# Attention, routed experts and a gated unit on one core: the gated unit's weight joins moved to steps 1 and 5 of an expert unit, the next inputs turned in step 7

## The chip, the core and the metric

The kernel runs on one core of one Trainium2 chip. A core has a matrix engine (TensorE, PE in the views), a vector engine (VectorE, DVE), a scalar engine (ScalarE, ACT), GpSimd (POOL) and a queue engine that issues most transfers (SyncE, SP). Every engine has its own instruction list and works it off in order; it stops where an instruction needs something that another engine or a transfer has not delivered. The metric is the time of one execution on the device in microseconds (us); smaller is better.

## The reference, cut to what matters

The kernel computes three layers on 4608 tokens of width 512. Only the second, with the beginning of the third, is near the change.

```
# 1: attention in chunks of 64 -> x (4608 x 512)
# 2: routed experts, each token goes to one of eight
do_compute = x @ w_skip > 0
e_idx = argmax(x[do_compute] @ w_gate);  gate_w = softmax at e_idx
for e in range(8):
    h = maximum(xc[mask] @ w1[e], 0)           # 512 -> 1024
    y[mask] = gate_w * (h @ w2[e])             # 1024 -> 512
x[do_compute] += y
# 3: gated unit on all tokens
silu = g * sigmoid(g),  g = x @ w_gate;  out = (silu * (x @ w_val)) @ w_out
```

Experts' and gated unit's matmuls are done in three passes: each operand is split into a high part and a low part (`hi`, `lo`), and hi*hi, lo*hi and hi*lo are added up (`mm3`, lines 250 to 252).

## The kernel before, in words

The experts' work is a list of eleven **units**, run one after the other: eight static units (one expert each, up to 272 tokens in two tiles of 128 rows and one of 16) and three dynamic units (128 tokens of an expert that is known only at run time). In order, with the number u: 0, 1, 2 static, 3 dynamic, 4 to 8 static, 9 and 10 dynamic. Unit 0 stands ahead of the loop that the change touches.

A static unit has eight **steps** (`f` = 0 to 7 in the code; the text says step 1 to 8). A step is: twelve matmuls of the first layer for 128 hidden columns into the PSUM tile `hp`; ScalarE takes the positive part as `hh`, VectorE makes the low part `hl` (line 394); then twelve matmuls of the second layer, of the step before, into the four tiles `yt`; then `tick(f)`, which appends side work. The second layer of step 8 is done in step 1 of the following unit. `back()` (in step 3) turns a finished unit's result `yts` on TensorE, and VectorE adds it to the tokens' rows (line 334).

The side work of `tick`, in the order in which it is written:

- `put` (step 4): three scatters of the unit before, issued by GpSimd (line 342).
- `gather(u + 1)` (step 2): the next unit's rows, up to three, issued by GpSimd (line 291).
- `xpose(u + 1)`: those rows are turned on TensorE into `tp` and one `hp` tile (line 322), ScalarE makes `xh`, VectorE `xl` (line 325).
- `pump`: slices of the coming experts' weights are split: ScalarE `whi` (line 148), then VectorE `wlo`, or GpSimd for every fourth slice (line 150). A static unit splits 16 slices, two or three in a step and one in steps 4 and 8. Its loads `st` go through SyncE's queue, in turn, each waiting for one of four buffers.
- `gpump`: one slice of the gated unit's weights, which lie in memory as 64-bit numbers, is **joined**: three VectorE instructions (lines 228, 231, 234) make `cv` from `gst`. `gsplit` then splits `cv`: ScalarE `ghi` (line 202), GpSimd `glo` (line 203). `gfetch` issues the load of the next `gst`, for which there is one buffer. Twelve slices are joined in the static units 1, 2 and 4 to 7, two in each.

`gpump` itself begins with a `gsplit` of whatever was joined before and is not yet split. No planner decides the order: each engine's list is in the order of the calls. Each of the PSUM tiles `hp` has two buffers, used in turn by the steps' first layer, by `back` and by `xpose`, so that a user waits until the one two places earlier has been read.

Of the kernel before, what the change touches and what calls it, by code (L numbers as in the profile page):

```python
# [54 lines left out]
def attention_moe_glu_kernel(  # L55
# [33 lines left out]
    gst = {"slice": 0, "dma": 0, "stage": [], "conv": []}  # L89
# [89 lines left out]
    def chunk_done(c):  # L179
        st["done"] = max(st["done"], c + 1)  # L180
# [18 lines left out]
    def gsplit():  # L199
        if gst["conv"]:  # L200
            w, hi, lo = gst["conv"].pop()
            nc.scalar.activation(out=hi, in_=w.bitcast(F32), func=ACTF.Copy)
            nc.gpsimd.tensor_tensor(out=lo, in0=w.bitcast(F32), in1=hi.bitcast(F32), op=ALU.subtract)
# [61 lines left out]
    def load_perm(u, bases):  # L265
        r = []
        for t, b in enumerate(bases):
            pm = al["pm"](u)
            idx = pm
            if t == 2:  # L270
                src = perm[b:b + REST, ROW - 2:]
                idx = al["pm"](u)[0:REST]
                ins = nc.sync.dma_start(out=idx, in_=src)
                after(ins, scattered)
                pm = pm[rest(u)]
            else:
                src = perm[b:b + P, ROW - 2:] if isinstance(b, int) else perm[bass.ds(b, P), ROW - 2:]
            ins = nc.sync.dma_start(out=pm, in_=src)
            after(ins, scattered)
            r.append([pm, idx])  # L280
        rows[u] = r
# [6 lines left out]
    def gather(u, n=NT + 1):  # L288
        for t, r in enumerate(rows[u]):
            x = al["x"](u) if t < 2 else al["xr"][rest(u)]  # L290
            ins = nc.gpsimd.indirect_dma_start(
                out=x, out_offset=None, in_=X[0:n, :],
                in_offset=bass.IndirectOffsetOnAxis(ap=r[1][:, 0:1].bitcast(U32), axis=0),
                bounds_check=n - 1, oob_is_err=False,
            )
            apart(ins, u)
            r.append(x)
# [12 lines left out]
    def xpose(u):  # L310
        xh, xl = xts[u] = al["xt"](u)
        for t, (_, _, x) in enumerate(rows[u]):
            n = P
            one = ident
            if t < 2:
                p = al["t"](t)
            else:
                p = al["h"](KD * P).rearrange("p (k t) -> p k t", k=KD)
                n = REST
                one = ident[rest(u), rest(u)]  # L320
            for k in range(KD):
                nc.tensor.transpose(p[:, k, 0:n], x[:, k * P:(k + 1) * P], one)
            sl = slice(t * P, t * P + n)
            nc.scalar.activation(out=xh[:, :, sl], in_=p[:, :, 0:n], func=ACTF.Copy)
            nc.vector.tensor_tensor(
                out=xl[:, :, sl], in0=p[:, :, 0:n], in1=xh[:, :, sl].bitcast(F32), op=ALU.subtract
            )
# [623 lines left out]
    with mctx:  # L951
        wb = gpool["b"] = ctx.enter_context(tc.tile_pool(name="wb", bufs=GSLOTS))
        gpool["t"] = ctx.enter_context(tc.tile_pool(name="cv", bufs=2))
        gpool["st"] = mctx.enter_context(tc.tile_pool(name="gst", bufs=1))
        hp_.append(mctx.enter_context(tc.tile_pool(name="hd", bufs=4)))
        ps_h = mctx.enter_context(tc.tile_pool(name="ps_h", bufs=2, space=PSUM))
        ps_y = mctx.enter_context(tc.tile_pool(name="ps_y", bufs=1, space=PSUM))
        ps_t = mctx.enter_context(tc.tile_pool(name="ps_t", bufs=2, space=PSUM))
        warm = io.tile([P, 1], F32, tag="warm", name="warm", bufs=1)
        al.update(  # L960
            t=lambda t: ps_t.tile([P, KD, P], F32, tag="t", name="tp"),
            h=lambda n: ps_h.tile([P, n], F32, tag="h", name="hp"),
            yt=lambda d: ps_y.tile([P, UNIT], F32, tag=f"y{d}", name="yt"),
            ts=lambda: hp_[1].tile([P, 2, UNIT], F32, tag="hd", name="yts"),
            y=lambda t: ps_y.tile([P, DM], F32, tag="y3", name="y"),
        )
        usual = dict(al)
        held = outs[:]
        outs.clear()
        al.update(  # L970
            pm=lambda u: io.tile([P, 2], I32, tag="lpm", name="lpm", bufs=1),
            x=lambda u: gpool["st"].tile([P, DM], F32, tag="st", name="lx"),
            xt=lambda u: [gpool["t"].tile([P, KD, P], F32R, tag="cv", name=nm) for nm in ("lxh", "lxl")],
        )

        total = nc.values_load(tab[0:1, 2 * TAB:], min_val=NDYN, max_val=TAB)
        with tc.For_i(NDYN, total, 1) as j:
            er = nc.values_load(tab[0:1, bass.ds(j, 1)], engines=[mybir.EngineType.SP], min_val=0, max_val=NE - 1)
            br = nc.values_load(
                tab[0:1, bass.ds(j + TAB, 1)], engines=[mybir.EngineType.SP], min_val=0, max_val=PERM - P  # L980
            )
            load_perm("loop", [br])
            gather("loop")
            xpose("loop")
            got = {}

            def getl(kind, h):
                i = (kind, h)
                if i not in got:
                    src = moe_src(er, kind, h)  # L990
                    hi = wb.tile([P, 4, 512], F32R, tag="w", name="wl_hi")
                    lo = wb.tile([P, 4, 512], F32R, tag="w", name="wl_lo")
                    t = wb.tile([P, 4, 512], F32, tag="w", name="wl")
                    nc.sync.dma_start(out=t, in_=src)
                    for k in range(KD):
                        nc.scalar.activation(out=hi[:, k, :], in_=t[:, k, :], func=ACTF.Copy)
                        nc.gpsimd.tensor_tensor(
                            out=lo[:, k, :], in0=t[:, k, :], in1=hi[:, k, :].bitcast(F32), op=ALU.subtract
                        )
                    got[i] = (hi, lo)  # L1000
                return got[i]

            unit_dyn("loop", getl, lambda kind, h: None, None, lambda f: None)()
            put()

        al.update(usual)
        outs.extend(held)
        put()
        gfetch()
        tail = None  # L1010
        for u, (kind, n) in enumerate(units):
            if not u:
                continue
            nxt = u + 1 < len(units)

            def tick(f, u=u, kind=kind, nxt=nxt):
                if f == (3 if kind == "s" else 2):
                    put()
                if f == 1 and kind == "s":
                    gather(u + 1)  # L1020
                if f == (5 if kind == "s" else 3) and nxt:
                    xpose(u + 1)
                if kind == "s":
                    pump(2 + f % 2)
                    if f in (2, 6) and gst["stage"]:
                        gpump(1)
                    if f in (0, 4) and gst["slice"] < 12:
                        gfetch()
                    if f == 4:
                        gsplit()  # L1030
                    if f == 6 and units[u + 1][0] == "d" and u + 2 < len(units):
                        gather(u + 2)
                elif nxt or f < 4:
                    pump(2)
                if u == len(units) - 2 and f == 3:
                    first_rows("a")
                if not nxt:
                    if f == 2:
                        gpool["ahead"] = 2
                        gfetch()  # L1040
                    elif f == 5:
                        xpose("a")
                        gpump(1)
                        nc.scalar.activation(out=warm, in_=ident[:, 0:1], func=ACTF.Sigmoid)
                if f == 3:
                    pre_perm(u + 3)

            fn = unit_static if kind == "s" else unit_dyn
            order = ORDER_S if kind == "s" else ORDER_D
            tail = fn(  # L1050
                u,
                lambda a, h, u=u, order=order: chunk(4 * u + order.index((a, h))),
                lambda a, h, u=u, order=order: chunk_done(4 * u + order.index((a, h))),
                tail, tick,
            )
        tail()
        put()
        gpool["ahead"] = 3
        gfetch()
# [151 lines left out]
```

## Time and profile before

| what | value |
|---|---|
| runs | 1342.19, 1343.88 and 1346.43 us; median 1343.88 |
| profiled execution | 1347.4 us, of it 1345.7 us from the first to the last instruction (the span) |
| TensorE | 1290.9 us busy, 96% of the span |
| VectorE | 647.2 us busy, 48% |
| ScalarE | 417.6 us busy, 31% |
| GpSimd | 256.0 us busy, 19% |
| mean granted TensorE clock | 0.988 |

The profiled execution is 3.5 us over the median. The shares of busy time are means over stages with different limits: up to about 190 us attention, routing and unit 0, from there to about 426 us the units 1 to 10, and then the gated unit. What a wait costs has to be read in its stage.

### The profile page before, as it was taken

What the parts mean: (1) busy time and instruction counts of PE and PEld (TensorE: products, weight loads), DVE (VectorE), ACT (ScalarE), POOL (GpSimd) and SP (SyncE); (2) the same over time, 40 slices, a digit from 0 to 9 for tenths busy, and PEclk for the clock granted to TensorE, in tenths of its full rate; (3) what the DMA queues carried; (4) which work ended last, traced back from release to release, by engine and by line L of the source; (5) the groups of instructions that cost most, each with busy time, mean ns of one, the idle gap of its engine ahead of it and who ended that gap; (6) DMA issues with size and microseconds to landing.
All of it is one profiled execution on the core that took longest, in us unless ns stands there. A gap on an engine that the chain in (4) does not pass through costs nothing.

```text
span 1345.7 us, 23671 instructions
## 1 busy us (share of the span) xinstructions
PE 1290.9 (96%) x9772; PEld 1192.8 (89%) x9772; DVE 647.2 (48%) x1159; ACT 417.6 (31%) x862; POOL 256.0 (19%) x226
## 2 busy tenths in 40 slices
PE   7688899999999999999999999999999999999998
PEld 6566699899997889999999999999999999999997
DVE  6688467687758885232333323332333333232332
ACT  4455345655555333121122212121212112111221
POOL 0156454555545563000000000000000000000000
PEclk9899799999999999999999999999999999999999
DMA  9996356786657441102020110202020100201000
GB/s 333 350 404 249 105 161 212 253 266 231 213 186 255 135 151 30 40 0 48 1 47 1 30 19 1 47 1 48 0 48 0 34 14 0 48 0 39 1 24 17
DMA packets 125904, 136.09 MB, mean 101 GB/s; under 512 B 78359, under 2 KB 81670, under 8 KB 125794
## 3 DMA queue, kind: packets, MB, share of 16 engines
q1 hardware_dynamic: 121090, 124.46, 29.0%
q0 software_dynamic: 4704, 10.10, 2.1%
q8 instruction: 77, 1.26, 0.4%
q14 instruction: 33, 0.27, 0.1%
HBM read 108.05 MB, written 27.17 MB: 100 GB/s over the span
## 4 chain that ended last, share of the span: by engine, by line
PE 76%; DVE 3%; issue 2%; ACT 2%; POOL 1%; DMA 1%; SPq 0%; POOLq 0%; ACTq 0%; DVEq 0%
PE o L252 7%; PE o L251 7%; PE o L250 7%; PE pg L252 7%; PE pg L250 7%; PE pg L251 7%; PE pv L252 7%; PE pv L251 7%; PE pv L250 7%; PE hp L250 2%; PE hp L252 2%; PE hp L251 2%; PE yt L251 2%; PE yt L252 2%; PE yt L250 2%
## 5 line engine op out<-in xcount | busy, mean ns | idle before, releaser
L1152 DVE TENSOR_TENSOR sg<-pg,sg 128x384 f32<-128x384 f32 (+1 forms) x132 | 72.1, 546 | 327.0 <-ACT sg L1151 327.0
L252 PE MATMUL pg<-xh,glo 128*128 128x384 f32 (+1 forms) x528 | 175.5, 332 | 0.0
L250 PE MATMUL pg<-xh,ghi 128*128 128x384 f32 (+1 forms) x528 | 175.1, 332 | 0.0
L1156 ACT ACTIVATE uh<-sg 128x384 fp32r<-128x384 f32 (+1 forms) x156 | 78.1, 500 | 311.9 <-DVE sg L1153 311.9
L251 PE MATMUL pg<-xl,ghi 128*128 128x384 f32 (+1 forms) x528 | 174.8, 331 | 0.0
L250 PE MATMUL pv<-xh,ghi 128*128 128x384 f32 (+1 forms) x528 | 173.9, 329 | 0.0
L251 PE MATMUL pv<-xl,ghi 128*128 128x384 f32 (+1 forms) x528 | 173.9, 329 | 0.0
L252 PE MATMUL pv<-xh,glo 128*128 128x384 f32 (+1 forms) x528 | 173.9, 329 | 0.0
L252 PE MATMUL o<-ghi,ul 128*128 128x512 f32 x432 | 171.1, 396 | 2.2 <-POOL ul L1158 2.2
L250 PE MATMUL o<-ghi,uh 128*128 128x512 f32 x432 | 168.8, 391 | 2.6 <-ACT uh L1156 2.6
L251 PE MATMUL o<-glo,uh 128*128 128x512 f32 x432 | 170.6, 395 | 0.0
L1151 ACT ACTIVATE sg<-pg 128x384 f32<-128x384 f32 (+1 forms) x132 | 63.6, 482 | 311.5 <-PE pg L252 311.5
L1153 DVE TENSOR_TENSOR sg<-pv,sg 128x384 f32<-128x384 f32 (+1 forms) x132 | 72.1, 546 | 118.4 <-PE pv L252 118.3
L1158 DVE TENSOR_TENSOR ul<-sg,uh 128x384 fp32r<-128x384 f32 (+1 forms) x132 | 72.2, 547 | 76.8 <-ACT uh L1156 76.8
L150 DVE TENSOR_TENSOR wlo<-st,whi 128x512 fp32r<-128x512 f32 x117 | 95.5, 844 | 27.2 <-ACT whi L148 23.0
L150 POOL TENSOR_TENSOR wlo<-st,whi 128x512 fp32r<-128x512 f32 x59 | 79.1, 1342 | 135.9 <-ACT whi L148 116.7
L250 PEld LDWEIGHTS pg<-xh,ghi 128*128 128x128 f32 x528 | 99.4, 188 | 5.9
L251 PEld LDWEIGHTS pg<-xl,ghi 128*128 128x128 f32 x528 | 99.3, 188 | 5.7
L148 ACT ACTIVATE whi<-st 128x512 fp32r<-128x512 f32 x176 | 101.8, 627 | 6.1 <-DMA st<-in_moe_w_dram 5.8
L252 PEld LDWEIGHTS o<-ghi,ul 128*128 128x128 f32 x432 | 81.0, 188 | 21.6 <-POOL ul L1158 4.4
L250 PEld LDWEIGHTS pv<-xh,ghi 128*128 128x128 f32 x528 | 99.3, 188 | 0.0
L251 PEld LDWEIGHTS pv<-xl,ghi 128*128 128x128 f32 x528 | 99.3, 188 | 0.0
(180 smaller groups left out, 2503.3 us busy)
## 6 DMA issues: line engine op xcount, KB each, us to landing
st<-in_moe_w_dram SPq DMA_DIRECT2D x88, 512.0 KB
q<-in_qkv_dram SPq DMA_DIRECT2D x35, 768.0 KB
X<-x SPq DMA_DIRECT2D x36, 256.0 KB
out_dram<-os SPq DMA_DIRECT2D x36, 256.0 KB
xr<-X SPq DMA_DIRECT2D x128, 64.0 KB
gst<-in_moe_w_gate_dram SPq DMA_DIRECT2D x12, 512.0 KB
gst<-in_moe_w_val_dram SPq DMA_DIRECT2D x12, 512.0 KB
gst<-in_moe_w_out_dram SPq DMA_DIRECT2D x12, 512.0 KB
```

The source lines that it names most:

```text
L148: nc.scalar.activation(out=hi[:, k, :], in_=stage[:, k % 2, :], func=ACTF.Copy)
L150: eng.tensor_tensor(out=lo[:, k, :], in0=stage[:, k % 2, :], in1=hi[:, k, :].bitcast(F32), op=ALU.subtract)
L250: nc.tensor.matmul(ps, ah, bh, start=start, stop=False)
L251: nc.tensor.matmul(ps, ah, bl, start=False, stop=False)
L252: nc.tensor.matmul(ps, al, bh, start=False, stop=stop)
L1151: nc.scalar.activation(out=u, in_=pg, func=ACTF.Sigmoid)
L1152: nc.vector.tensor_tensor(out=u, in0=pg, in1=u, op=ALU.mult)
L1153: nc.vector.tensor_tensor(out=u, in0=pv_, in1=u, op=ALU.mult)
L1156: nc.scalar.activation(out=uh, in_=u, func=ACTF.Copy)
L1158: eng.tensor_tensor(out=ul, in0=u, in1=uh.bitcast(F32), op=ALU.subtract)
```

## The change

Three of `tick`'s conditions change. The next inputs are turned in step 7 in place of step 6. A slice is joined in steps 1 and 5 in place of 3 and 7. The next slice is fetched in steps 3 and 7 in place of 1 and 5, and the separate `gsplit` goes from step 5 to step 3. Nothing is added or taken away.

```
-                if f == (5 if kind == "s" else 3) and nxt:
+                if f == (6 if kind == "s" else 3) and nxt:
                     xpose(u + 1)
                 if kind == "s":
                     pump(2 + f % 2)
-                    if f in (2, 6) and gst["stage"]:
+                    if f in (0, 4) and gst["stage"]:
                         gpump(1)
-                    if f in (0, 4) and gst["slice"] < 12:
+                    if f in (2, 6) and gst["slice"] < 12:
                         gfetch()
-                    if f == 4:
+                    if f == 2:
                         gsplit()
                     if f == 6 and units[u + 1][0] == "d" and u + 2 < len(units):
                         gather(u + 2)
```

VectorE's list from the turned inputs of unit 6 through the first three steps of unit 7; `hl` are the low parts of the steps, the three `cv` rows are one join. Before:

```order
L325 TENSOR_TENSOR xl<-hp,xh 128x4x16
L150 TENSOR_TENSOR wlo<-st,whi 128x512 x2
L394 SCALAR_TENSOR_TENSOR hl<-hp,hh 128x272
L150 TENSOR_TENSOR wlo<-st,whi 128x512 x2
L228 TENSOR_SCALAR cv<-gst 128x512
L231 SCALAR_TENSOR_TENSOR cv<-gst,cv 128x512
L234 SCALAR_TENSOR_TENSOR cv<-gst,cv 128x512
L394 SCALAR_TENSOR_TENSOR hl<-hp,hh 128x272 x2
L150 TENSOR_TENSOR wlo<-st,whi 128x512 x2
L394 SCALAR_TENSOR_TENSOR hl<-hp,hh 128x272
```

The same place of the changed kernel:

```order
L325 TENSOR_TENSOR xl<-hp,xh 128x4x16
L150 TENSOR_TENSOR wlo<-st,whi 128x512 x2
L394 SCALAR_TENSOR_TENSOR hl<-hp,hh 128x272 x2
L150 TENSOR_TENSOR wlo<-st,whi 128x512 x2
L228 TENSOR_SCALAR cv<-gst 128x512
L231 SCALAR_TENSOR_TENSOR cv<-gst,cv 128x512
L234 SCALAR_TENSOR_TENSOR cv<-gst,cv 128x512
L394 SCALAR_TENSOR_TENSOR hl<-hp,hh 128x272
```

The join stood ahead of the `hl` pair of step 8 and the next unit's step 1; now it stands behind this pair and ahead of the `hl` of step 2. The turned inputs are one step nearer to the unit's end.

GpSimd's list in a unit like 7, from the gather of the next unit's rows on; `wlo` are its shares of the experts' weights. Before:

```order
L291 DMA x<-X,pm 128x512 x2
L291 DMA xr<-X,pm 16x512
L150 TENSOR_TENSOR wlo<-st,whi 128x512
L203 TENSOR_TENSOR glo<-cv,ghi 128x512
L342 DMA X<-x,pm 4609x512 x2
L342 DMA X<-xr,pm 4609x512
L150 TENSOR_TENSOR wlo<-st,whi 128x512
L203 TENSOR_TENSOR glo<-cv,ghi 128x512
L150 TENSOR_TENSOR wlo<-st,whi 128x512 x2
```

The same unit of the changed kernel:

```order
L203 TENSOR_TENSOR glo<-cv,ghi 128x512
L291 DMA x<-X,pm 128x512 x2
L291 DMA xr<-X,pm 16x512
L150 TENSOR_TENSOR wlo<-st,whi 128x512
L203 TENSOR_TENSOR glo<-cv,ghi 128x512
L342 DMA X<-x,pm 4609x512 x2
L342 DMA X<-xr,pm 4609x512
L150 TENSOR_TENSOR wlo<-st,whi 128x512 x3
```

One `glo` now stands ahead of the gathers, and both stand ahead of the scatters; behind the scatters the three shares of `wlo` follow one another.

## Rows read from the trace of the kernel before

**Rows 1.** Busy time by engine in stretches, in us; PEclk is the granted clock.

```profile
190.00:430.00 240.00, 231.98 (x1729) 221.03 (x1727) 172.67 (x263) 133.96 (x282) 122.35 (x98) 0.99 0.70 231
430.00:530.00 100.00, 94.59 (x655) 86.47 (x654) 79.01 (x118) 32.20 (x72) 58.16 (x46) 1.00 0.40 123
```

**Rows 2.** Waits of TensorE from 190 to 430 us: total, times, longest.

```profile
PE yt L251 <- DVE hl L394: 2.8, 5, 0.8
```

**Rows 3.** Timeline of TensorE, unit 7's step 1: start, duration, instruction, idle before it.

```profile
342.85 0.28 PE L252 MATMUL hp<-xh,wlo 128*128 128x272 f32 x1
342.97 0.29 PE L250 MATMUL yt<-hh,whi 128*128 128x272 f32 x1
343.74 0.40 PE L251 MATMUL yt<-hl,whi 128*128 128x272 f32 x1 [0.48 <-DVE hl L394]
343.98 0.29 PE L252 MATMUL yt<-hh,wlo 128*128 128x272 f32 x1
```

**Rows 4.** Timeline of TensorE, unit 4's step 5.

```profile
274.14 0.29 PE L250 MATMUL yt<-hh,whi 128*128 128x272 f32 x1
...
275.49 0.29 PE L252 MATMUL yt<-hh,wlo 128*128 128x272 f32 x1
```

**Rows 5.** Timeline of VectorE from unit 6's turned inputs to unit 7's step 1.

```profile
336.51 0.21 DVE L325 TENSOR_TENSOR xl<-hp,xh 128x64 fp32r<-128x64 f32 x1
...
341.67 1.67 DVE L234 SCALAR_TENSOR_TENSOR cv<-gst,cv 128x512 uint32<-128x512 uint32 x1
343.26 0.78 DVE L394 SCALAR_TENSOR_TENSOR hl<-hp,hh 128x272 fp32r<-128x272 f32 x2
```

**Rows 6.** The tile gst, 190 to 430 us: duration ns min/median/max, first and last start.

```profile
L228 DVE TENSOR_SCALAR cv<-gst x14: 411/416/1118, 202.9 to 428.2; 128x512 uint32<-128x512 uint32 x14
...
L234 DVE SCALAR_TENSOR_TENSOR cv<-gst,cv x14: 691/693/2066, 204.1 to 429.3; 128x512 uint32<-128x512 uint32 x14
```

**Rows 7.** Timeline of VectorE, one join in unit 4.

```profile
270.91 1.12 DVE L228 TENSOR_SCALAR cv<-gst 128x512 uint32<-128x512 uint32 x1 [0.32 <-DMA gst<-in_moe_w_val_dram]
...
272.79 2.07 DVE L234 SCALAR_TENSOR_TENSOR cv<-gst,cv 128x512 uint32<-128x512 uint32 x1
```

**Rows 8.** Timeline of GpSimd beside that join.

```profile
270.37 1.37 POOL L203 TENSOR_TENSOR glo<-cv,ghi 128x512 fp32r<-128x512 f32 x1 [2.20 <-ACT ghi L202]
...
272.98 1.31 POOL L150 TENSOR_TENSOR wlo<-st,whi 128x512 fp32r<-128x512 f32 x1
```

**Rows 9.** Timeline of ScalarE in unit 7, steps 1 and 6.

```profile
345.72 1.15 ACT L148 ACTIVATE whi<-st 128x512 fp32r<-128x512 f32 x2
...
360.22 0.40 ACT L393 ACTIVATE hh<-hp 128x272 fp32r<-128x272 f32 x1 [1.04 <-PE hp L252]
```

**Rows 10.** Timeline of VectorE in unit 7, steps 1 and 5.

```profile
346.37 1.29 DVE L150 TENSOR_TENSOR wlo<-st,whi 128x512 fp32r<-128x512 f32 x2 [2.33 <-ACT whi L148]
...
358.17 1.54 DVE L150 TENSOR_TENSOR wlo<-st,whi 128x512 fp32r<-128x512 f32 x2
```

**Rows 11.** Timeline of TensorE in unit 7: `back` in step 3, `xpose` in step 6.

```profile
350.60 0.60 PE L377 MATMUL hp<-ident,yts 128*16 128x128 f32 x4
...
361.53 1.03 PE L322 MATMUL tp<-ident,x 128*128 128x128 f32 x8
```

**Rows 12.** Timeline of GpSimd in unit 7: gathers, scatters, a share of `wlo`.

```profile
342.95 1.34 POOL L291 DMA_INDIRECT x<-X,pm  x1 [0.16 <-issue]
...
345.91 0.90 POOL L291 DMA_INDIRECT xr<-X,pm  x1 [0.30 <-issue]
...
353.41 1.31 POOL L342 DMA_INDIRECT X<-x,pm  x1 [0.15 <-issue]
...
357.23 1.32 POOL L150 TENSOR_TENSOR wlo<-st,whi 128x512 fp32r<-128x512 f32 x1
```

**Rows 13.** Timeline of SyncE's queue in unit 4: issue of a `gst` load.

```profile
262.92 0.46 SPq L193 DMA_DIRECT2D gst<-in_moe_w_val_dram  x1
```

**Rows 14.** Chain that ended last, 405 to 420 us: a load from issue to landing.

```profile
413.08 4.85 DMA st<-in_moe_w_dram
```

## The prediction

> **What bounds the kernel now.** I read first the busy time by stretch, since the change lies between 190 and 430 us alone. There TensorE is busy 232.0 of 240.0 us at a granted clock of 0.99, and VectorE 172.7 [rows 1]. So TensorE's own work sets this stretch, its instructions are the same after the change, and all that can be won are its waits, some 8 us. Then the waits of TensorE: one group belongs to the units and comes back, five waits of the second layer's second matmul (which reads `hl`) for VectorE, 2.8 us by the view [rows 2]. The others are single events at the stretch's ends, which the change does not touch. Behind the stretch the gated unit has TensorE busy for 94.6 of 100 us [rows 1] and takes over a shift of the stretch's end one to one.
>
> Then the timeline at such a wait. In unit 7's step 1 the matmul on `hh` starts at 342.97, the one on `hl` only at 343.74, and the third at 343.98 [rows 3]. At the usual pitch of 0.125 us (342.85 to 342.97 in the same rows) the third would start 0.25 us after the first. It starts 1.01 after it: the wait costs 0.76 us, more than the 0.48 of idle time that the row shows. Four of the five waits are of this kind, at the beginning of units 2, 6, 7 and 8. The fifth is in unit 4: 275.49 - 274.14 - 0.25 = 1.10 us [rows 4]. **All five: 4 x 0.76 + 1.10 = 4.14 us**, 0.31% of the time, and the most that the change can win.
>
> Last, why `hl` is late. VectorE finishes the turned inputs at 336.72, is then in arrears with `wlo`, and the join's last instruction takes 1.67 us instead of 0.69, so that the `hl` pair begins at 343.26 only [rows 5, 6].
>
> **Unknown that decides: two engines that shut each other out.** The join's instructions take 0.41, 0.69 and 0.69 us when nothing disturbs them [rows 6]. Beside a GpSimd split they don't share, they wait. In unit 4 a first join instruction that began at 270.91, inside a GpSimd split that ended at 271.74, ended at 272.03, 0.3 us behind it. A last one begun at 272.79 ended at 274.86, 0.57 us after the split of 272.98 to 274.29 [rows 7, 8]. So each meeting costs VectorE about 1 us, and the order of GpSimd's list matters as much as that of VectorE's.
>
> The Trainium skill, "SBUF — State Buffer", section "Who interferes with whom", says that a VectorE instruction with two inputs in SBUF contends with a GpSimd one that reads SBUF, that whichever issues first keeps the shared ports for its whole length, and that the other fully blocks. The rows agree that one blocks; but the instruction of 272.79 is recorded 0.19 us ahead of GpSimd's and was nevertheless the one that waited. What the page's order of precedence would make of the sum is the rival "half".
>
> **The change part by part,** on unit 7's times of before.
>
> *Turning in step 7.* Moved behind two groups of twelve matmuls, 24 x 0.125 = 3.0 us. Its matmuls are the same ones. VectorE is then done with `xl` at 336.72 + 3.0 = 339.7, two `wlo` (1.29 for two [rows 10]) bring it to 341.0, and `hl` of step 8, 0.4 long [rows 5], is done near 341.4. TensorE wants it at 342.97 + 0.125 = 343.1. No join stands between any more. The wait is covered by 1.7 us, and the next unit's first matmul at 341.47 finds `xl` ready. **Gain: 0.76 us at the start of units 2, 6, 7 and 8.** In unit 4 the join of step 3 goes too: **1.10 us**.
>
> *Joining in step 1.* From here on TensorE stands 0.76 us earlier than in the rows. ScalarE's two `whi` of step 1 end at 345.72 + 1.15 - 0.76 = 346.1 [rows 9], and `ghi`, the same operation on a tile of the same size (half of 1.15, 0.6 us), now follows at once, to 346.7. VectorE's two `wlo` end at 346.37 + 1.29 - 0.76 = 346.9 [rows 10] and the join begins. But at 346.7 GpSimd begins `glo`, some 1.4 us long (1.37 and 1.32 in [rows 8, 12]), to 348.1. The first join instruction therefore ends some 0.3 us behind it, at 348.4; with 2 x 0.69, gaps, and 0.4 for `hl` (half of 0.78 [rows 5]), step 2's `hl` is done near 350.3. Queued behind it on VectorE stand the next `wlo` and `hl`; waiting for it is TensorE, since the last four transposes of `back`, at 350.60 - 0.76 = 349.84 [rows 11], go into the `hp` buffer of step 2, which is free when that `hl` has read it. The wait is 0.45 us, and starting again costs another 0.1 (from 343.74 to 343.98 in [rows 3] it is 0.24 in place of 0.125); without the meeting it is nothing, with one more of 0.2 to 0.3 it is 0.75. I take 0.6. `back` with a pending `glo` and a join exists in units 2, 5, 6 and 7. **Loss: 4 x 0.6 = 2.4 us**, between 0 and 3.0.
>
> *Joining in step 5.* What is late here is GpSimd's list. Before, the gathers start at 342.95 and end at 346.81, 3.86 us; the scatters start at 353.41 and the split behind them at 357.23, 3.82 us [rows 12]. Now, end to end: `glo` to 348.1 and hand-over to 348.2, gathers to 352.1, a split to 353.5, the second `glo` to 354.9, scatters to 358.75, and the split of 357.23 runs from 358.75 to about 360.3, 1.6 us later than before. VectorE's two `wlo` of step 5 (358.17 to 359.71 before [rows 10]) end about 359.4, and the join's first instruction meets this split: done near 360.7, the second near 361.4. ScalarE begins step 6's slices behind `hh`, which ends at 360.62 [rows 9], some 0.15 earlier now; two `whi` later, at 361.55, GpSimd starts its next split, and the last join instruction meets that one: 361.55 + 1.3 + 0.57 = 363.4, and `hl` of step 6 is done at 363.9. TensorE has no turned inputs here any more, so its step 7 begins at 361.53 - 0.15 = 361.4 [rows 11], and after twelve matmuls, 1.5 us, it wants `hl` at 363.0. **Loss: about 0.95 us** in the units where gathers, `back` and scatters are all there in full: 5, 6 and 7, **2.85 us**. Unit 2 gathers one tile and unit 4 scatters one, so that GpSimd is some 2.6 us earlier; unit 1 has no `back`. I take nothing there.
>
> *Fetching in steps 3 and 7.* The load of step 3 now stands in SyncE's list behind a weight load that waits for a buffer until VectorE has split step 3's first slice, near 355.5, and the join of step 5 wants it at 359.4 to 360.7. A load took 4.85 us from issue to landing at 413.08 [rows 14]; the `gst` issued at 262.92 [rows 13] held VectorE's join up until 270.91 [rows 7], 8.0 us. Issued at 355.9 the first lands at 360.75, just in time; the second at 363.9. The rows don't say which is nearer; I take the first, since it asks no queue of transfers ahead beyond one load, at no cost; by the second `hl` would be done at 366.1, and the wait 3.1 us in place of 0.95. The load of step 7 has about 7 us and is covered.
>
> *Sum:* -4.14 + 2.4 + 2.85 = **+1.1 us** on the profiled 1347.4 us, whose span is 1345.7. That execution is 3.5 us over the median 1343.88, on which I put the same sum: **1345.0 us**. Five waits go, seven smaller or equal ones come.
>
> **The rivals.**
> - *Half: the step 5 meetings don't happen.* If the join's last instruction, begun at 361.45, keeps GpSimd out instead of being kept out, `hl` of step 6 is done at 362.6, before 363.0. -4.14 + 2.4 = -1.7, 1342.1 us. For it: a shift of the two lists by 0.2 us is enough. Against it: the instruction of 272.79, which began first and waited [rows 7, 8]. The page's precedence named above leads to this one.
> - *All gain: the step 1 meeting doesn't reach TensorE either*, because `glo` or the join comes half a microsecond later or earlier than I reckon. -4.14, 1339.7 us. Against it: two engines' lists send `glo` and the join off within 0.2 us.
> - *Slower: the `gst` load of step 3 lands late.* Place: step 5 of units 5 to 7, VectorE idle ahead of line 228. It decides from a landing about 361 us on. At 8.0 us the sum is -4.14 + 2.4 + 3 x 3.1 = +7.6, 1351.5 us; at 6 us, +4 or so. For it: the landing of 8.0 us [rows 7, 13], and the scatters that run in the same 4 us. Against it: the 4.85 us [rows 14].
>
> **How the numbers follow.** A difference of 0.3%, 4.0 us, is about what a measurement of this kernel can tell from none: its three runs lie 4.2 us apart. Chances: waits change place (1345.0, between 1343 and 1347) 0.40; half 0.25; all gain 0.12; late load 0.23. Faster by over 0.3% is most of the upper end of "all gain", 0.09; slower by over 0.3% a good half of the late load, 0.14; within it 0.77. The range 1340.0 to 1350.0 leaves out half of "all gain" and the far end of the late load. The likeliest case alone: 1343 to 1347.
>
> **What would show it.** In the profile after: no wait for `hl` of step 8 at the start of units 2, 6, 7 and 8, and none in unit 4's step 5 (if they are there, the first step is wrong). Waits of 0.4 to 0.75 us at the transposes of `back`, line 377, in units 2, 5, 6, 7. Waits of about 1 us at line 251 in step 7 of units 5, 6, 7, with the join's last instruction at 1.5 us or more beside a GpSimd split. Line 228 idle for `gst` at most a few tenths. What would make the prediction wrong: a landing past 361 us, or meetings that fall otherwise by 0.3 us, since in both places the margin is smaller than that.

## The result: 15 us slower, outside the range

| | before | after |
|---|---|---|
| device time, median of 5 runs | 1342.19 us (1339.98 to 1346.43) | 1357.18 us (1354.09 to 1357.29) |
| ratio to before, 95% interval | 1 | 1.0107 (1.0092 to 1.0121) |
| profiled execution: time, span | 1347.4, 1345.7 us | 1354.09, 1352.3 us |
| first matmul of unit 1 to first matmul of the gated unit | 234.05 us | 247.56 us |

The change costs 15.0 us; 1345.0 was forecast, and the range ended at 1350. The two profiled executions lie only 6.7 us apart, because the attention ahead of the experts, which the change leaves alone, took 6.4 us longer in the profile of before (unit 1 begins there at 192.84, after the change at 186.48). So I compare the stretch from unit 1's first matmul to the first of the gated unit, which holds everything that was moved. Two lines on TensorE's timeline of the changed kernel bound it: start, duration, instruction, idle before it.

```profile
186.48 0.39 PE L250 MATMUL hp<-xh,whi 128*128 128x272 f32 x1 [2.04 <-issue]
...
434.04 0.28 PE L250 MATMUL pgv<-xh,ghi 128*128 128x256 f32 x1
```

It is 13.5 us longer than in the profile of before (192.84 to 426.89). Both kernels were profiled once more (below): 234.46 and 251.02 us, 16.6 apart. The two differences average 15.0 us, which happens to be that of the medians too; what sets the two pairs apart is told with the clock further down. The loss lies in this stretch.

Next the waits of TensorE in it, which answer to [rows 2]: total, times, longest, in the changed kernel.

```profile
PE yt L251 <- DVE hl L394: 8.8, 5, 2.5
PE y L250 <- ACT hth L428: 3.0, 1, 3.0
PE hp L377 <- DVE hl L394: 2.1, 4, 1.5
...
PE hp L250 <- DVE hl L394: 0.5, 1, 0.5
```

The first row looks like the one of before with three times the total, 8.8 in place of 2.8, and again five waits. They are five other waits: none stands at the start of a unit or in unit 4's step 5 any more, and all five are in step 7, in units 2, 4, 5, 6 and 7. One of them, on TensorE in unit 7:

```profile
366.12 0.29 PE L250 MATMUL yt<-hh,whi 128*128 128x272 f32 x1
368.69 0.40 PE L251 MATMUL yt<-hl,whi 128*128 128x272 f32 x1 [2.29 <-DVE hl L394]
368.93 0.29 PE L252 MATMUL yt<-hh,wlo 128*128 128x272 f32 x1
```

Read as [rows 3] were, it costs 368.93 - 366.12 - 0.25 = 2.56 us. VectorE's timeline says what made `hl` late:

```profile
361.25 2.72 DVE L150 TENSOR_TENSOR wlo<-st,whi 128x512 fp32r<-128x512 f32 x2
...
366.40 0.43 DVE L228 TENSOR_SCALAR cv<-gst 128x512 uint32<-128x512 uint32 x1 [2.44 <-DMA gst<-in_moe_w_out_dram]
...
367.59 0.69 DVE L234 SCALAR_TENSOR_TENSOR cv<-gst,cv 128x512 uint32<-128x512 uint32 x1
368.20 0.43 DVE L394 SCALAR_TENSOR_TENSOR hl<-hp,hh 128x272 fp32r<-128x272 f32 x1
```

VectorE stands idle for 2.44 us ahead of the join's first instruction, for the transfer of `gst`; behind it the join runs undisturbed (0.43 and 0.69 are its free durations, [rows 6]), and only then comes the `hl` that TensorE waits for. SyncE's list has the issue of this load, behind two weight loads:

```profile
356.92 2.16 SPq L137 DMA_DIRECT2D st<-in_moe_w_dram  x2
359.13 0.46 SPq L193 DMA_DIRECT2D gst<-in_moe_w_out_dram  x1
```

From 359.13 to 366.40 are 7.3 us, not the 4.85 of [rows 14]. VectorE's waits over the whole stretch show that this is no single case; before, there was one such wait, of 0.3 us:

```profile
DVE cv L228 <- DMA gst<-in_moe_w_val_dram: 3.7, 2, 2.6
DVE cv L228 <- DMA gst<-in_moe_w_gate_dram: 2.5, 2, 1.6
DVE cv L228 <- DMA gst<-in_moe_w_out_dram: 2.4, 1, 2.4
```

Five waits, 8.6 us, against five of TensorE with 8.8.

**The sum from these traces.** The five old waits saved 4.14. The new ones cost, from start to start as in the prediction, 1.52 (unit 2), 0.94 (unit 4), 2.73, 2.55 and 2.56 (units 5, 6, 7): 10.3. The matmuls right behind unit 6's wait took another 1.0 us, at a lower granted clock (further down): 11.3. The transposes of `back` cost 0.35 each in units 5, 6 and 7 and 2.45 in unit 2: 3.5. From unit 8's last `back` to the gated unit's first matmul it takes 28.03 us in place of 25.78: 2.25. Together -4.14 + 11.3 + 3.5 + 2.25 = 12.9 of the 13.5; the other 0.6 I did not assign. For one whole unit the same shows as a pitch: from `back` to `back` 27.5 us before, 29.85, 31.0 and 29.7 after (units 5 to 8).

### The profile page after: what moved, and what is told of

It is laid out like the page before. It is cut to its first block, busy times and chain, and to the rows that moved or that the text cites. A ratio compares the mean times of both kernels' runs of the same rounds, so it can differ in the third digit from the quotient of the medians.

```text
span 1352.3 us, 23663 instructions
## 1 busy us (share of the span) xinstructions
PE 1288.8 (95%) x9772; PEld 1192.5 (88%) x9772; DVE 649.9 (48%) x1159; ACT 418.6 (31%) x862; POOL 254.1 (19%) x226
## 4 chain that ended last, share of the span: by engine, by line
PE 73%; DVE 4%; DMA 3%; issue 3%; ACT 1%; POOL 1%; SPq 0%; DVEq 0%; POOLq 0%; ACTq 0%
PE o L252 7%; PE o L251 7%; PE o L250 7%; PE pg L252 7%; PE pg L250 7%; PE pg L251 7%; PE pv L251 7%; PE pv L252 7%; PE pv L250 7%; PE hp L250 2%; PE hp L252 1%; PE hp L251 1%; PE yt L251 1%; PE yt L252 1%; DVE wlo L150 1%
## 5 line engine op out<-in xcount | busy, mean ns | idle before, releaser
L150 DVE TENSOR_TENSOR wlo<-st,whi 128x512 fp32r<-128x512 f32 x117 | 98.5, 877 | 24.4 <-ACT whi L148 23.4
L252 PEld LDWEIGHTS pv<-xh,glo 128*128 128x128 f32 x528 | 99.3, 188 | 0.0
```

Source lines behind the costliest of these rows:

```text
L150: eng.tensor_tensor(out=lo[:, k, :], in0=stage[:, k % 2, :], in1=hi[:, k, :].bitcast(F32), op=ALU.subtract)
L252: nc.tensor.matmul(ps, al, bh, start=False, stop=stop)
```

## The experiments

The change moves four conditions of `tick`: turning, join, fetch and separate split. The theory after this reading: the load of `gst`, fetched in steps 3 and 7, comes too late for the join of step 5. The rivals: (A) the meetings of VectorE's join with GpSimd's splits make `hl` late, and the wait for the load only takes up time that would be lost anyway; (B) the turning in step 7 does it, since it leaves TensorE nothing to do between `hh` and `hl` of step 6.

**e1: the change, with the fetch where it was before.**

```diff
-                    if f in (2, 6) and gst["slice"] < 12:
+                    if f in (0, 4) and gst["slice"] < 12:
                         gfetch()
```

> The changed kernel with the fetch of the next slice back in steps 1 and 5, right behind the join that frees the buffer, so that the load is issued four steps ahead of its join. Theory (late load: the load issued in step 3 lands about 7 us later, VectorE stands at the join of step 5 and TensorE in step 7): the waits of step 7, 11.3 us in units 2 and 4 to 7 of the changed kernel's trace, go; 1342 to 1346 us, near the kernel before. Rival A (VectorE and GpSimd shutting each other out, as the prediction had it): the step 5 meetings stay, 1345 to 1349 us. Rival B (turning in step 7 is what delays): still 1353 to 1358 us.

Measured: 1346.66 us, 1.0033 (1.0020 to 1.0046) against before. That is outside the theory's range and in A's. One pair of numbers that says in which steps a load is sent off gives back 10.5 of the 15 us (9.9 by the two ratios). The timelines of SyncE, VectorE and GpSimd in unit 7:

```profile
344.70 0.34 SPq L193 DMA_DIRECT2D gst<-in_moe_w_out_dram  x1
```

```profile
352.70 2.69 DVE L150 TENSOR_TENSOR wlo<-st,whi 128x512 fp32r<-128x512 f32 x2
...
356.49 1.67 DVE L234 SCALAR_TENSOR_TENSOR cv<-gst,cv 128x512 uint32<-128x512 uint32 x1
```

```profile
356.33 1.29 POOL L150 TENSOR_TENSOR wlo<-st,whi 128x512 fp32r<-128x512 f32 x1 [1.49 <-issue]
```

The load now leaves 10.6 us ahead of its join (line 228 starts at 355.31), and no wait for it is left on VectorE. What is left is what the prediction described in step 5: the join's last instruction, 1.67 us in place of 0.69, beside a GpSimd split that began at 356.33. It makes TensorE wait in step 7, by 1.02, 1.00 and 1.00 us in units 5, 6 and 7; 0.95 was forecast. So the theory holds for 10.5 us, and A is right too, for some 3 us that appear when the load is on time; after the change the late load hides these meetings, since the join then runs behind the splits. With the 3.5 us at `back` the sum is -4.14 + 3.0 + 3.5 = +2.4; measured +3.9 (2.7 to 6.2 by the interval).

**e2: the change, with eleven of the twelve `gst` loads left out.**

```diff
         while gst["dma"] <= min(gst["slice"] + gpool["ahead"], 35):
             c, k = divmod(gst["dma"], 4)
+            if 0 < gst["dma"] < 12:
+                gst["stage"].append(gst["one"])
+                gst["dma"] += 1
+                continue
...
+            gst["one"] = t
             gst["stage"].append(t)
```

> The changed kernel, in which eleven of the twelve loads of gated slices in the units are left out: all twelve joins read the slice that was loaded first (so part of the gated unit's first weights is left out). Late load: VectorE can't wait for the landing, 1341 to 1345 us, and at most 2 us better than with the early fetch, by what the loads cost on the shared transfers. Rival A: 1345 to 1349 us. Rival B: 1353 to 1358 us.

Measured: 1345.21 us, 1.0019 (1.0007 to 1.0032). That is just above the 1341 to 1345 of "late load", and again in A's range. Without the loads 12 us of the loss go, 1.5 more than by sending them off earlier, and the intervals of the two runs overlap. So it is their lateness that costs; that their traffic costs anything is not shown. The wait at `hl` is 2.3 us in three waits, as in e1 (2.2 in three).

**e3 and e4: the two halves of the change alone.** e3 is the change with the turning back in step 6, e4 the kernel before with the turning alone moved to step 7.

```diff
-                if f == (6 if kind == "s" else 3) and nxt:
+                if f == (5 if kind == "s" else 3) and nxt:
                     xpose(u + 1)
```

> Joins, fetches and the separate split moved as in the change, the next inputs turned in step 6 as before. Late load: VectorE's wait for the landing stays, 1352 to 1358 us. Rival A: 1345 to 1350. Rival B: back near 1342 us or a little below.

> Only the turning moved to step 7, joins and fetches as in the kernel before. Late load: nothing is fetched late, but the join of step 7 now stands directly behind the low parts of the turned inputs, so that the wait for step 8's low part at the units' starts becomes 1 to 1.5 us in place of 0.76: 1342 to 1347 us. Rival B: 1353 to 1358 us.

Measured: e3 1357.93 us, 1.0118 (1.0093 to 1.0144); e4 1345.59 us, 1.0015 (1.0003 to 1.0026). The joins and fetches alone cost all that the change costs, and B falls. The waits of TensorE, then of VectorE, in e3:

```profile
PE hp L250 <- DVE hl L394: 10.4, 5, 4.6
```

```profile
DVE cv L228 <- DMA gst<-in_moe_w_out_dram: 5.0, 2, 3.3
DVE cv L228 <- DMA gst<-in_moe_w_gate_dram: 3.6, 3, 1.9
...
DVE cv L228 <- DMA gst<-in_moe_w_val_dram: 3.3, 3, 2.1
```

With the turning in step 6 TensorE has work between `hh` and `hl` and doesn't wait at line 251; it waits a little later, at an `hp` buffer that the same late `hl` must have read. That cover shifts the wait and doesn't shorten it. In e4, where the old join of step 7 still stands ahead of `hl`, the turning alone makes the old waits longer; TensorE's row of waits, and VectorE's timeline ahead of unit 7:

```profile
PE yt L251 <- DVE hl L394: 5.9, 6, 1.3
```

```profile
337.77 1.75 DVE L231 SCALAR_TENSOR_TENSOR cv<-gst,cv 128x512 uint32<-128x512 uint32 x1
...
340.17 0.78 DVE L394 SCALAR_TENSOR_TENSOR hl<-hp,hh 128x272 fp32r<-128x272 f32 x2
```

They are 1.1 to 1.5 us each in place of 0.76, 7.4 from start to start in place of 4.14. That is +3.2, and the time is up by 2.85 (2.0 by the ratio, 0.4 to 3.5). Half of the change, the later turning, helps only when the join is gone from where it was.

**e5 and e9: what makes the load take 7.3 us?** The scatters run just then. e5 is the change with `put`, which issues them, moved from step 4 to step 6, e9 with it in step 7.

```diff
-                if f == (3 if kind == "s" else 2):
+                if f == (5 if kind == "s" else 2):    # e9: 6
                     put()
```

> The changed kernel with the scatters of the unit before issued in step 6 in place of step 4, so that they no longer run beside the gated load of step 3. If the scatters are what stretches its landing from about 4.3 us (as the same load takes in the kernel before) to 7, VectorE's wait in step 5 falls by 2 us or more a unit: 1344 to 1349 us. If the weight loads issued just ahead of it are the cause, it stays: 1353 to 1358 us. If the meetings of VectorE and GpSimd were the cause, GpSimd's split of step 4 comes some 4 us earlier and the gain is under 1 us a unit: 1350 to 1355 us.

> The changed kernel with the scatters issued in step 7, behind GpSimd's split of step 6, so that they begin after the gated load of step 3 should have landed. (With the scatters in step 6, the run before, GpSimd began them 0.9 us after that load's issue, where they had begun 0.8 us ahead of it, so that they still ran beside it, and the landing took 6.4 us in place of 7.2.) If the scatters stretch the landing, it takes 4 to 5 us, and what is left in step 7 is the 1.0 us of the meetings: 1344 to 1349 us. If the weight loads ahead of it do, the landing stays over 6 us: 1351 to 1357 us.

Measured: e5 1352.07 us, 1.0074 (1.0046 to 1.0102); e9 1352.91 us, 1.0074 (1.0054 to 1.0095). In e5, SyncE's list, then VectorE's, then GpSimd's:

```profile
356.01 0.46 SPq L193 DMA_DIRECT2D gst<-in_moe_w_out_dram  x1
```

```profile
362.39 0.43 DVE L228 TENSOR_SCALAR cv<-gst 128x512 uint32<-128x512 uint32 x1 [3.00 <-DMA gst<-in_moe_w_out_dram]
```

```profile
356.87 1.31 POOL L342 DMA_INDIRECT X<-x,pm  x1 [0.16 <-issue]
```

The scatters still began 0.86 us behind the issue, so that this run settled nothing about them; the landing took 6.4 us. The time lies in the range given to the meetings, but VectorE's waits for the load are still there, 10.9 us in five. Hence e9, in the same order:

```profile
359.58 0.46 SPq L193 DMA_DIRECT2D gst<-in_moe_w_out_dram  x1
```

```profile
357.69 3.13 DVE L150 TENSOR_TENSOR wlo<-st,whi 128x512 fp32r<-128x512 f32 x2
...
365.55 0.43 DVE L228 TENSOR_SCALAR cv<-gst 128x512 uint32<-128x512 uint32 x1 [2.59 <-DMA gst<-in_moe_w_out_dram]
```

```profile
367.42 1.31 POOL L342 DMA_INDIRECT X<-x,pm  x1 [0.15 <-issue]
```

Here the scatters began behind the landing, and it still took 6.0 us. So the scatters account for at most 1.3 of the 7.3 us. The other 1.1 to 1.2 over the 4.85 of [rows 14] belong to something else. SyncE issues two weight loads in the 2.2 us ahead of it, and in e8 (next) only one. VectorE doesn't wait there, but the traces hold every packet, and those of a `gst` load can be told by their size of 4 KB. From issue to the end of its last packet it takes 6.8, 6.2 and 6.7 us in units 5, 6 and 7 of the changed kernel, 6.0, 5.9 and 5.4 in e9, and 6.0, 4.2 and 4.2 in e8. In units 6 and 7 the second weight load goes with 1.2 to 1.7 us; unit 5 does not show it, and no run moved the weight loads alone. The time gained at the load, e9 partly lost again: the scatters' new place lets GpSimd's splits meet two `wlo` of VectorE (3.13 us for the pair of 357.69, 1.29 undisturbed in [rows 10]), and TensorE waits for the `hl` behind them, 0.66 to 0.69 us in units 5, 6 and 7.

**e7 and e8: what is left with the load on time.** e8 is the change with the fetch in steps 2 and 6; e7 is e1 with GpSimd's share of the experts' `wlo` given to VectorE.

```diff
-                    if f in (2, 6) and gst["slice"] < 12:
+                    if f in (1, 5) and gst["slice"] < 12:    # e8
```

```diff
-        eng = nc.gpsimd if n % 4 == 3 or not st["ahead"] else nc.vector
+        eng = nc.vector if st["ahead"] else nc.gpsimd    # e7, with the fetch of e1
```

> The changed kernel with the fetches in steps 2 and 6: the load moves ahead of one weight load in the queue and is issued some 1.8 us earlier, with one transfer less ahead of it. Late load: it lands 3 to 4 us earlier and the wait of 2.5 to 3.5 us in step 7 shrinks to the 1.0 us of the early fetch: 1344 to 1349 us. If not the load but the step in which things are joined counts: 1353 to 1358 us.

> The changed kernel with the early fetch (steps 1 and 5), in which VectorE makes all low parts of the experts' weights from unit 0 on, so that the join meets none of GpSimd's splits of expert weights. If meetings make the waits of 1.0 us in step 7 of units 5 to 7, they go, against some 0.7 us more of VectorE's work four times a unit: 1341 to 1346 us. If it is VectorE's amount of work, they grow: 1347 to 1353 us.

Measured: e8 1344.69 us, 1.0023 (1.0009 to 1.0037); e7 1344.40 us, 1.0016 (1.0001 to 1.0031). One step earlier than in the change is enough for the load: in e8 VectorE never waits for it, and the step 7 waits are 1.15, 1.01 and 1.00, close to those of e1. In e7 no GpSimd split is left for VectorE's join to meet in step 5, and the waits of TensorE are these:

```profile
PE hp L250 <- DVE hl L394: 1.2, 1, 1.2
...
PE hp L377 <- DVE hl L394: 0.7, 4, 0.2
```

The three waits of 1.0 us in step 7 are gone, which confirms the meetings as their cause. The median is 2.3 us under e1's, but the two intervals overlap.

**e6 and e10: the joins somewhere else.** If lateness of `hl` is the price of every join that stands ahead of an `hl`, the joins belong behind it in a step where VectorE has little to do. e6 is the kernel before with the joins in steps 4 and 8, e10 the same with `ghi` and `glo` sent off a step later, in 1 and 5. The turning is in step 6 and the fetch in steps 1 and 5, as before.

```diff
-                    if f in (2, 6) and gst["stage"]:
+                    if f in (3, 7) and gst["stage"]:    # e6, e10
                         gpump(1)
...
-                    if f == 4:
+                    if f in (0, 4):    # e10
                         gsplit()
```

> The kernel before with the joins in steps 4 and 8, where only one slice of expert weights is split and GpSimd does it; turning in step 6, fetches in steps 1 and 5 and the separate split in step 5 as before. By late load and by the meetings alike, the load has three steps or more, and the join stands behind the low part of step 4 or 8 and not ahead of it, with nothing on VectorE that the next low part is due for within 3 us: the five waits of the kernel before, 4.1 us, go and none comes, 1337 to 1341 us. If VectorE's total work and not its order makes the waits, 1342 to 1346 us.

> The kernel before with the joins in steps 4 and 8 (as in the run with joins there) and the separate split in steps 1 and 5, so that GpSimd's low part of the slice joined in step 8 is made in step 1 and not beside the join of step 4, where VectorE was kept out by two GpSimd splits in a row. If that pair makes the one wait that was left, 1.96 us in unit 4, it shrinks to under 1 us: 1338 to 1341 us, 3 us below the kernel before. If the late weight load of that unit makes it, 1340 to 1342 us.

Measured: e6 1340.86 us, 0.9989 (0.9976 to 1.0003), no difference that can be told (of the waits "none comes", but one came); e10 **1337.43 us, 0.9966 (0.9953 to 0.9978)**, 4.6 us under before. In e6 the join's second instruction meets two GpSimd splits, one right behind the other (VectorE, then GpSimd):

```profile
346.66 3.31 DVE L231 SCALAR_TENSOR_TENSOR cv<-gst,cv 128x512 uint32<-128x512 uint32 x1
```

```profile
346.86 1.31 POOL L150 TENSOR_TENSOR wlo<-st,whi 128x512 fp32r<-128x512 f32 x1
...
348.10 1.31 POOL L203 TENSOR_TENSOR glo<-cv,ghi 128x512 fp32r<-128x512 f32 x1
```

There it is covered, but in unit 4 a wait of 1.96 us is left. In e10 `glo` no longer follows the join, and TensorE's waits in the stretch are

```profile
PE y L250 <- ACT hth L428: 3.2, 1, 3.2
PE tp L425 <- DVE x L334: 0.6, 2, 0.3
PE o L252 <- POOL ul L1158: 0.5, 1, 0.5
PE tp L322 <- DVE htl L429: 0.3, 1, 0.3
```

with no wait for `hl` at all. The gain of 4.6 us is about the 4.14 that the prediction put on the five waits of before as the most there is. In the profiles, unit 1's first matmul to unit 8's last `back` takes 204.3 us in place of 208.3.

**e11 and e12: both kernels once more,** for a second profile of each.

> The kernel before once more, for a second profile. If the stretch from the last transposes of unit 8's result to the gated unit's first matmul (25.8 us in its first profile, 26.2 to 29.4 in those of all changed kernels) depends on the change, it is 25.8 again; if it depends on how transfers fall in an execution, it lies elsewhere in that span.

> The changed kernel once more, for a second profile. Late load: VectorE waits for the gated load in step 5 of units 4 to 7 again, and TensorE 2 to 4 us in step 7 of each; the units 1 to 10 take 12 to 15 us more than in the kernel before, while attention ahead of them differs by several us from execution to execution.

Measured: 1338.89 and 1355.16 us. The lines that bound the stretch, first in the kernel before, then in the changed one:

```profile
183.91 0.39 PE L250 MATMUL hp<-xh,whi 128*128 128x272 f32 x1 [2.04 <-issue]
...
418.37 0.28 PE L250 MATMUL pgv<-xh,ghi 128*128 128x256 f32 x1
```

```profile
184.13 0.39 PE L250 MATMUL hp<-xh,whi 128*128 128x272 f32 x1 [2.04 <-issue]
...
435.15 0.28 PE L250 MATMUL pgv<-xh,ghi 128*128 128x256 f32 x1
```

This time both begin within 0.22 us of each other, and the whole difference is in the stretch: 16.6 us, more than the 12 to 15 expected. The five waits of step 7 are there again, and a sixth of 1.24 us at the start of unit 1. From unit 8's last `back` on it is 26.1 us here in before and 27.5 after the change, so that the 2.25 of the first pair shrink to 1.4; in the other kernels it lies between 26.2 and 29.4, 28.2 in the fastest of all, e10. It goes with the granted clock: in four profiles (both of before, e1, e7) this part has 2.4 GHz throughout and takes 25.8 to 26.4 us; in the other ten TensorE is granted 1.2 GHz for 3.4 us of it, and it takes 27.4 to 29.4. The clock fell in the last 1.2 us of the one long wait there (`y` for `hth`, line 428) or up to 1.7 us behind it; this wait is 2.3 to 2.7 us in the four and 2.5 to 3.4 in the ten. What makes this wait longer or shorter stays open; e4, e6 and e10 have the lower clock there as well, so that it does not take the late load.

## Why the prediction was wrong

**The five old waits go: right,** all of them, for the 4.14 us reckoned; e10 shows from the other side that they were worth it.

**The step that failed is "Fetching in steps 3 and 7".** It put the issue at 355.9. The trace after has it at 359.13; unit 7 stands 3.44 us later in this trace by the prediction's own clock, so that the same instant is 355.7. The place in SyncE's list, and what holds it up there, were right. Wrong was "I take the first, since it asks no queue of transfers ahead beyond one load, at no cost": the landing took 7.3 us and not 4.85. Of the two rows that it had, the far one (8.0 us, [rows 7, 13]) was nearly right. The near one, the 4.85 of [rows 14], belongs to the first of three weight loads, behind two loads of `x`; SyncE's list in the kernel before, then the busy time over the 4.85 us:

```profile
412.01 0.82 SPq L304 DMA_DIRECT2D x<-X  x2
413.08 1.66 SPq L137 DMA_DIRECT2D st<-in_moe_w_dram  x3
```

```profile
413.08:417.93 4.85, 4.23 (x21) 3.16 (x19) 1.95 (x3) 0.00 (x0) 0.00 (x0) 1.00 0.94 316
```

The transfers were not quieter there: share 0.94 at 316 GB/s, against 0.90 at 305 from 359.0 to 366.5 after the change. What does differ is the place in the queue. In the second profile of before the first load of the same three took 5.0 us and the third 6.8; the load of 8.0 us had three weight loads in the 3.6 us ahead of it, the moved one two in 2.2 us, where the prediction counted one. That the queue is the cause is argued from these rows and e8, as said there. e1, e2 and e8 show that this step alone is worth 10.5 to 12.5 us by the medians, 9.9 to 11.8 by the ratios.

**The rival "late load" had the mechanism and too small a price.** For a landing of 8.0 us it gave a wait of 3.1 us in unit 7; by its own working 7.3 gives some 2.4, and 2.56 was measured. But it counted units 5, 6 and 7 only. I had excluded units 2 and 4 ("I take nothing there") because GpSimd has less to do in them, which is an argument on meetings; the load doesn't depend on it, and it cost 1.52 and 0.94 us there too. In unit 6 the wait and the matmuls right behind it cost 3.55, of which the wait is 2.55, and the rest is the clock's, for which the prediction has no term:

```profile
330.00:345.00 15.00, 12.88 (x91) 12.47 (x91) 9.58 (x16) 6.23 (x14) 3.81 (x4) 0.89 0.58 190
423.00:433.00 10.00, 7.79 (x32) 6.15 (x33) 5.48 (x9) 6.84 (x12) 3.82 (x3) 0.83 0.87 314
```

In these stretches of the changed kernel (length, busy us of the five engines, granted clock, share of the DMA engines, GB/s) the granted clock is 0.89 and 0.83: behind idle times of 2.1 us in unit 6 and 3.0 in unit 10 TensorE was granted the lower level, 1.2 GHz, for 3.4 us, from 337.4 and from 426.1. The pitch of unit 6 is 31.0 us and that of its neighbours 29.7 and 29.85, so it costs some 1.2 us more than they do. The idle 2.5 us of unit 5 left the clock alone in this profile; in e12 it fell behind the waits of units 5, 6 and 7 alike, and the pitches are 31.6, 30.9 and 31.0. That is 3.1 of the 4.0 us by which the second pair of profiles lies further apart than the first, up to unit 8's last `back`; the wait in unit 1 is most of the rest.

**Joining in step 5: right where it could be seen.** The meetings were forecast at 0.95 us each in units 5, 6 and 7 and cost 1.00 to 1.02 in e1 and 1.00 to 1.15 in e8. In the changed kernel itself the late load covers them.

**Joining in step 1: right in three units, missed in one.** On TensorE, then VectorE, then GpSimd, in unit 7 of the changed kernel:

```profile
353.65 0.61 PE L377 MATMUL hp<-ident,yts 128*16 128x128 f32 x4 [0.18 <-DVE hl L394]
```

```profile
350.27 1.52 DVE L228 TENSOR_SCALAR cv<-gst 128x512 uint32<-128x512 uint32 x1
...
353.16 0.43 DVE L394 SCALAR_TENSOR_TENSOR hl<-hp,hh 128x272 fp32r<-128x272 f32 x1
```

```profile
350.14 1.37 POOL L203 TENSOR_TENSOR glo<-cv,ghi 128x512 fp32r<-128x512 f32 x1 [4.20 <-ACT ghi L202]
```

The join meets `glo` as reckoned, and `back` waits at line 377; 0.35 us of cost in place of 0.6, and under the 0.4 that was to show it. Unit 2 cost 2.45: it gathers only one tile, so that GpSimd's next split follows soon and meets the join's last instruction as well (VectorE, then GpSimd):

```profile
219.69 2.02 DVE L234 SCALAR_TENSOR_TENSOR cv<-gst,cv 128x512 uint32<-128x512 uint32 x1
```

```profile
219.87 1.27 POOL L150 TENSOR_TENSOR wlo<-st,whi 128x512 fp32r<-128x512 f32 x1
```

Less work on GpSimd made it worse, since it brought the split forward into the join. In all 3.5 us in place of 2.4. The rival "half" ends with this: where the load is on time, in e1 and e8, each of the three meetings takes place.

With the measured sizes in its own sum the prediction would have read -4.14 + 3.5 + 10.3, +9.7 us; 1.0 is the clock's in unit 6, and 2.25 come from the end of the stretch, which it had not looked at: there too the clock has part, and the cause of the longer wait ahead of it stays open.

## What to carry to other kernels

When a load is moved within its queue, take for its landing a row in which as many loads stand close ahead of it in the queue as at the new place, and reckon every unit that makes the load, not those alone where the engines are crowded; if the two ends of its duration lie on both sides of the point that decides, it is the slow end that the forecast must carry. A wait of the engine that bounds the kernel can cost more than its length: where the granted clock fell behind one, the unit took 1.2 to 1.7 us more. Work that is to be cheap belongs behind the instruction that the bound engine waits for, and its partner on another engine a step away from it: moving the join behind `hl` and `glo` a step further won here what moving the join to another busy step could not.

## What the hardware showed that I had not expected

- An instruction of VectorE that started first still waited for a GpSimd split: it began at 346.66, the splits at 346.86 and 348.10, and it ended at 349.97, 0.56 us behind the second (e6). Two splits in a row take 0.69 us to 3.31. The Trainium skill, "SBUF — State Buffer", section "Who interferes with whom", says that the order of issue decides who blocks; by the recorded starts it is the other way here, as in [rows 7, 8].
- An operation with a single input in SBUF waits too: line 228 took 1.52 us beside `glo`, 0.41 undisturbed.
- The attention ahead of the experts took up to 9 us more or less in executions of one kernel (unit 1 began at 192.84 and at 183.91 in the two profiles of before). About half of the loss was hidden in the first pair of spans by that.
